# Near units' probabilities turned by VectorE and moved by DMA, with the order planned anew around the VectorE-GpSimd port

## The chip, the cores and the metric

One core of one Trainium2 chip. The metric is the device time of the program in microseconds. The kernel before took 573.14 us (median of three runs, 572.16 to 573.74).

## The reference

Block-sparse attention, then a channel mixer. q, k and v are (4, 8, 768, 64): 4 batches, 8 heads, 768 positions in 24 blocks of 32. A query block sees its own block and both neighbours, blocks 0 and 23, and three sampled blocks; query blocks 0 and 23 see everything.

```python
scores = np.where(mask, scale * q @ k.T, -1e9)
attn = np.exp(scores - scores.max(-1)); attn /= attn.sum(-1) + 1e-9
x = heads_side_by_side(attn @ v)                       # (4, 768, 512)
x_prev = shift_by_one_position(x)
xk = mu_k * x + (1 - mu_k) * x_prev;  xr = mu_r * x + (1 - mu_r) * x_prev
k = relu(xk @ w_k)                                     # (512, 1024)
out = sigmoid(xr @ w_r) * (k * k @ w_v)                # (1024, 512), (512, 512)
```

The three weights come as float64 and are made into float32 on the chip; q, k and v are float32.

## The kernel before

The work is cut into units and tiles. Units 0 to 3 (`wide_unit`) are query blocks 0 and 23 of one batch each, against all 768 keys. Units 4 to 25 (`near_unit`) are one query block each, n = 1 to 22, of all four batches, against eight key blocks per batch; a near unit is worked in two groups (`gi`) of four heads. The mixer has 12 tiles of two query blocks; tile t needs the near units of its two blocks.

A near group goes through these steps. TensorE makes the scores `s` (L559). VectorE takes the row maxima `nm` (L567, L569). ScalarE takes exp in four instructions into `p` (L539), with the columns of a 128 x 128 part so interleaved that part x holds the keys of all four batches. `turn` (L515) then transposes `p` in two halves: four TensorE transposes against the identity into PSUM tile `t` (L523), and one copy of 128 x 512 into `pt`, by ScalarE (L527) or VectorE (L529; one of four halves, from unit 6 on). TensorE multiplies `pt`, 32 x 32 at a time, by the values `VA` into `o` (L585). `finish` divides by the sums (L657 to L661), transposes (`tx`, L668) and copies into `xt` (L685, L688).

A mixer tile: `split_x` makes `xr` and `xk` (differences by GpSimd L740, VectorE L743, ScalarE L750, GpSimd L752) as high and low halves; `gate` (L776), `hidden` (L794) and `values` (L823) are TensorE products of three terms each; ScalarE and GpSimd square (L807 to L811), VectorE multiplies by the gate (L831), SyncE stores (L834). Products, `t` and `tx` share two PSUM banks, tag "m". `weight` makes each of 20 weight pieces float32 (L373 to L392) and splits it (L396, L400).

Nothing is in a fixed order: each piece is given to `Plan.add` with an engine, an estimated duration, a rank (a due time in us, such as `UNIT_AT`, `MIX_AT` plus an offset such as `O_PV`), what it reads and writes, and buffers. `Plan.order` simulates the engines: on each engine, of the pieces that could start within `NEAR` ns of the first, the one of lowest rank is taken. The pieces are then emitted in that order, and every engine, SyncE's DMA queue too, runs its own in order. All loads and stores are issued by SyncE.

```python
HOP = {"PE": 260, "ACT": 100, "DVE": 170, "POOL": 170, "SP": 60}
late, op, at = min((c for c in cand if c[0] <= first + NEAR),
             key=lambda c: (c[1].rank - STAY * (c[1].table is not None and c[1].table == now_on), c[1].seq))
```

Of the kernel before, what the change touches and what calls it, by code (L numbers as in the profile page):

```python
# [81 lines left out]
class Op:  # L82
    __slots__ = ("engine", "ns", "lag", "fn", "rank", "deps", "users", "bufs", "end", "start", "table", "seq", "waits", "release", "size", "code", "dmas")


class Plan:


    HOP = {"PE": 260, "ACT": 100, "DVE": 170, "POOL": 170, "SP": 60}
    SWITCH = {"ACT": 1300, "PE": 110}  # L90
    SAME = {"PE": 0}
    RING, RING_POOL, RATE, DONE, DONE_POOL = 650, 1000, 370, 670, 2600
# [7 lines left out]
    def add(self, engine, ns, rank, fn, reads=(), writes=(), lag=0, table=None, release=0.0, size=0, code=0, dmas=1):  # L100
# [36 lines left out]
    CHUNK, FIRST, FETCHED, FLIGHT = 258, 214, 5200, 8  # L137

    def feed(self, op, at, ns):

        end, left, since = at, op.code, self.crossed
        upto = self.upto
        while left >= upto:
            end += ns * upto / op.code
            end = since = max(end, since + self.FETCHED)
            left -= upto
            upto = self.CHUNK
        return end + ns * left / max(op.code, 1), since, upto - left

    WINDOW, LOW, HIGH = 3413.0, 0.45, 0.75  # L150
# [39 lines left out]
    def order(self):  # L190
        free, table, avail = {}, {}, {}
        self.crossed, self.upto = 0.0, self.FIRST
        self.now, self.busy, self.speed, self.window_end = 0.0, 0.0, 1.0, self.WINDOW
        queue_free, lands = 0.0, [0.0] * self.FLIGHT
        for op in self.ops:
            if not op.waits:
                avail.setdefault(op.engine, []).append(op)
# [3 lines left out]
        while len(placed) < len(self.ops):  # L201
            best = None
            for engine, ops in avail.items():
                now = free.get(engine, 0.0)
                cand = []
                for op in ops:
                    at = max(now, op.release)
                    if op.size and engine != "POOL":
                        at = max(at, lands[-self.FLIGHT])
                    for d in op.deps:  # L210
                        at = max(at, d.end + (self.HOP[d.engine] if d.engine != engine else self.SAME.get(engine, 60)) + d.lag)
# [7 lines left out]
                    if at is not None:  # L219
                        cand.append((at + (self.feed(op, at, op.ns)[0] - at - op.ns if op.code else 0.0), op, at))  # L220
                if cand:
                    first = min(c[0] for c in cand)
                    now_on = table.get(engine)
                    late, op, at = min((c for c in cand if c[0] <= first + NEAR),
                                 key=lambda c: (c[1].rank - STAY * (c[1].table is not None and c[1].table == now_on), c[1].seq))
# [20 lines left out]
            for buf in op.bufs:  # L246
# [7 lines left out]
                if not buf.left:  # L254
                    self.queues[buf.tag][1].append((op.end + op.lag + self.HOP[op.engine], buf.slot))
            for u in op.users:
                u.waits -= 1
                if not u.waits:
                    avail.setdefault(u.engine, []).append(u)
            placed.append(op)  # L260
        return sorted(placed, key=lambda o: o.start)

# [9 lines left out]
def block_sparse_attention_channel_mix(  # L272
# [18 lines left out]
    plan.add(POOL, 400, -9, lambda: make_identity(nc, ident.ap), writes=[(ident,)])  # L291
# [10 lines left out]
    def mask_setup():  # L302
# [35 lines left out]
        plan.add(DVE, 4000, PICK + 3, pack, reads=[(number,), (con,)], writes=[(r,), (e,), (packed,)])  # L338
# [19 lines left out]
    def weight(i, owner, key, dst, src, rank):  # L358
        f = buf([P, 512], F32, "zr", 3, f"wf{i}")
        if wide:  # L360
# [7 lines left out]
            if i in MAG_POOL:  # L368
                plan.add(POOL, 1950, rank, lambda: nc.gpsimd.tensor_scalar(
                    out=mag.ap, in0=raw.ap[:, :, 1].bitcast(F32), scalar1=2.0**-111, scalar2=None, op0=ALU.mult),  # L370
                    reads=[(raw,)], writes=[(mag,)])
            else:
                plan.add(ACT, 690, rank, lambda: nc.scalar.activation(  # L373
# [16 lines left out]
            plan.add(DVE, 500, rank, shift, reads=[(mag,)], writes=[(mag,)])  # L390
            plan.add(DVE, 800, rank, sign, reads=[(mag,), (raw,)], writes=[(mag,)])
            plan.add(DVE, 800, rank, tail, reads=[(mag,), (raw,)], writes=[(f,)])  # L392
        else:
            plan.add(SP, ISSUE, rank, lambda: nc.sync.dma_start(f.ap, src), writes=[(f,)], size=262144)
        if i in HI_POOL:
            plan.add(POOL, 700, rank, lambda: nc.gpsimd.tensor_copy(dst()[:, 0, :], f.ap), reads=[(f,)], writes=[(owner, (0, key))])  # L396
        else:
            plan.add(ACT, 520, rank, lambda: nc.scalar.copy(dst()[:, 0, :], f.ap), reads=[(f,)], writes=[(owner, (0, key))])
        plan.add(POOL, 1300, rank,
                 lambda: nc.gpsimd.tensor_tensor(out=dst()[:, 1, :], in0=f.ap, in1=dst()[:, 0, :], op=ALU.subtract),  # L400
                 reads=[(f,), (owner, (0, key))], writes=[(owner, (1, key))])
# [113 lines left out]
    def turn(parts, name, rank, engine=ACT):  # L515

        tp = buf([P, 4, P], F32, "m", M_BUFS, f"t{name}", ps)
        pt = buf([P, 4, P], F32, "pt", PT_BUFS, f"pt{name}")
        many = len(parts)

# [4 lines left out]
        plan.add(PE, 98 * many, rank, tr, reads=[(ident,), *[(p, x // P // 3 if wide_p(p) else x // 256) for p, x in parts]], writes=[(tp,)], code=2 * many)  # L525
        if engine == ACT:
            plan.add(ACT, 200 + 0.75 * P * many, rank + 0.1, lambda: nc.scalar.copy(pt.ap[:, 0:many], tp.ap[:, 0:many]), reads=[(tp,)], writes=[(pt,)])  # L527
        else:
            plan.add(DVE, 150 + 1.05 * P * many, rank + 0.1, lambda: nc.vector.tensor_copy(out=pt.ap[:, 0:many], in_=tp.ap[:, 0:many]), reads=[(tp,)], writes=[(pt,)])  # L529
        return pt  # L530
# [6 lines left out]
    def direct_exp(p, out, s, view, nm, rank, key, turned=lambda x: x):  # L537
        width = out.stop - out.start
        plan.add(ACT, 262 + 0.83 * width, rank, lambda: nc.scalar.activation(  # L539
            turned(p.ap[:, out]), view(), AF.Exp, bias=nm(), scale=SCALE), reads=[(s,), key[0]], writes=[(p, key[1])], table="exp")  # L540

    def near_unit(at, q, first, o, t0, kind):

        c0 = first // QB
        for gi in range(2):
# [4 lines left out]
            p = buf([P, 4 * 256], F32, "p", P_BUFS, f"p{name}")  # L550
# [20 lines left out]
            plan.add(DVE, N_TOP, t1 + O_MAX[kind], top, reads=[(s,)], writes=[(nm,)])  # L571
            for i in range(4):
# [3 lines left out]
                           lambda one: one.rearrange("p (c x j) -> p c j x", c=2, j=QB))  # L576
            pts = [turn([(p, x * P) for x in range(4 * k, 4 * k + 4)], f"{name}_{k}", t1 + O_TR[kind], DVE if at >= TURN_FROM and (gi, k) in TURN_DVE else ACT) for k in range(2)]

            def pv(pts=pts, gi=gi):
                for row in range(2):  # L580
                    for a in range(2):
                        i, h = 2 * a + row, 4 * gi + 2 * a + row
                        for g in range(2):
                            for j in range(QB):
                                nc.tensor.matmul(  # L585
                                    o[gi].ap[ROWS[j], i * DV : (i + 1) * DV], pts[row].ap[:, 2 * a + g, ROWS[j]],
                                    VA.ap[:, c0 + g, j, h * DV : (h + 1) * DV], start=(g == 0), stop=(g == 1), skip_group_check=True)

            plan.add(PE, N_PV, t1 + O_PV[kind], pv, reads=[(x,) for x in pts] + [(VA, *PLACE(c0, *range(QB)), *PLACE(c0 + 1, *range(QB)))],
                     writes=[(o[gi], 0)], table="values", code=128)  # L590

    def wide_unit(b, q, o, t0, kind):

        W = S // 2
        for i in range(2):
# [4 lines left out]
            for k in range(2):  # L600
# [11 lines left out]
                plan.add(PE, N_WIDE_S, t1, mm, reads=[(q,), (KA, *wide_key_parts(b, i), *wide_key_parts(b, i + 2))], writes=[(s,)], table="wide", code=16)  # L612
                plan.add(DVE, 930, t1 + O_MAX[kind], lambda s=s, k=k, nm=nm: nc.vector.tensor_reduce(
# [6 lines left out]
            plan.add(DVE, 220, t1 + O_MAX[kind], top, reads=[(nm, 0, 1)], writes=[(nm, 2)])  # L620
            pp = [buf([P, 4 * 256], F32, "p", P_BUFS, f"p{name}_{row}") for row in range(2)]
            wide_ps.update(pp)
            for k in range(2):
                for row in range(2):
                    direct_exp(pp[row], slice(k * W, (k + 1) * W), ss[k], lambda s=ss[k], row=row: s.ap[:, row, 0:W],
                               lambda nm=nm, row=row: nm.ap[:, 2, row : row + 1], t1 + O_EXP[kind], ((nm, 2), k))
            parts = [(p, n * P) for p in pp for n in range(6)]
            pts = [turn(parts[4 * k : 4 * k + 4], f"{name}_{k}", t1 + O_TR[kind] + 0.05 * k) for k in range(3)]
            for row in range(2):

                def pv(row=row, i=i, pts=pts):
                    c = 2 * i + row
                    for n in range(6):
                        x = 6 * row + n
                        c1, part = wide_place(b, n)
                        for a in range(2):
                            h = 4 * a + c
                            for e in range(2):
                                nc.tensor.matmul(
                                    o.ap[ROWS[2 * a + e], c * DV : (c + 1) * DV], pts[x // 4].ap[:, x % 4, ROWS[2 * a + e]],  # L640
# [3 lines left out]
                plan.add(PE, N_WIDE_PV, t1 + O_PV[kind], pv, reads=[(pts[k],) for k in (row, row + 1)]  # L644
# [3 lines left out]
    def finish(at, members, o, parts, rank):  # L648
# [3 lines left out]
        for i in range(len(o)):  # L652
# [7 lines left out]
            plan.add(DVE, 366, rank, recip, reads=[(o[i], *parts)], writes=[(R, i)])  # L660
            plan.add(DVE, 420, rank, lambda i=i, each=each: nc.vector.tensor_tensor(  # L661
# [8 lines left out]
        plan.add(PE, 200 * len(o), rank, tr, reads=[(x, *range(len(o))), (ident,)], writes=[(tp,)], code=4 * len(o))  # L670
        n = members[0][1]
        if not n:
# [9 lines left out]
            plan.add(ACT, 1100, rank, put, reads=[(tp,)], writes=[(xt[0], ("w", b)), (xt[NTILE - 1], ("w", b))])  # L682
            return
        to = tile_of(n // 2)
        plan.add(ACT, 600, rank, lambda: nc.scalar.copy(  # L685
            to.ap[:, :, n % 2, :, 1:], tp.ap.rearrange("p c (b x) -> p c b x", b=B)), reads=[(tp,)], writes=[(to, n)])
        then = tile_of((n + 1) // 2)
        plan.add(ACT, 240, rank + 0.1, lambda: nc.scalar.copy(  # L688
# [9 lines left out]
    def attention():  # L698
        for t in (0, NTILE - 1):
            tile_of(t)  # L700
        plan.add(POOL, 50, -5, lambda: nc.gpsimd.memset(xt[0].ap[:, :, 0, :, 0:1], 0.0), writes=[(xt[0], ("z", 0))])
# [261 lines left out]
```

## Time and profile before

| what | value |
|---|---|
| median of three runs | 573.14 us (572.16 to 573.74) |
| span of the profiled execution, first to last instruction | 570.2 us |
| mean granted TensorE clock | 0.987 of 2.4 GHz |
| read and written in HBM | 78.60 MB, 6.29 MB |

The profiled execution has no own time beside its span; the median of the runs is 2.9 us above the span. In the views, PE is TensorE's matmuls, PEld its weight loads, DVE VectorE, ACT ScalarE, POOL GpSimd, SPq SyncE's queue. The chain follows the work that ended last back from the end, at each step to what released it. Matmuls overlap one another, so that a piece of the chain tells better than a mean duration what an instruction costs TensorE.

### The profile page before, as it was taken

The page shows a single profiled execution, that of the slowest core. Times are in us where ns is not written, and L with a number is a line of the kernel's source. Part 1 is how long each engine was busy: PE and PEld are TensorE (multiplying, and loading weights), DVE is VectorE, ACT ScalarE, POOL GpSimd, SP SyncE. Part 2 cuts the span into 40 slices and gives each one's busy share as a digit, 9 for nine tenths or more (in the row PEclk, how much of TensorE's full clock was granted, in tenths as well). Part 3 has the DMA queues.
Part 4 walks back from the last instruction along what each step waited for, and adds up shares of the span by engine and source line. Part 5 has one row for each costly group of instructions (what it writes and reads, how often), then busy time and mean ns, then how long its engine had stood idle before and what let it go on. Part 6 is the DMA issues. An engine that isn't in the chain of part 4 may idle for free.

```text
span 570.2 us, 18311 instructions
## 1 busy us (share of the span) xinstructions
PE 537.7 (94%) x7724; PEld 438.5 (77%) x7724; DVE 269.6 (47%) x533; ACT 325.2 (57%) x612; POOL 291.0 (51%) x359
## 2 busy tenths in 40 slices
PE   6788778979999999999999999999999999999997
PEld 2454556856887798897798798887877989889886
DVE  0877998887445353434424524433452242142411
ACT  0676687768478468467464756546564356424330
POOL 0430456887266066346066285373383663448752
PEclk9799899999999999999999999999999999999999
DMA  8999899773653553362651804135510302110001
GB/s 314 395 398 342 295 343 352 260 228 94 192 182 95 172 164 116 112 189 76 189 167 29 278 24 157 36 100 166 169 39 20 95 19 84 32 39 1 20 20 38
DMA packets 34183, 86.09 MB, mean 151 GB/s; under 512 B 5010, under 2 KB 5780, under 8 KB 31124
## 3 DMA queue, kind: packets, MB, share of 16 engines
q1 hardware_dynamic: 34100, 84.92, 44.5%
q8 instruction: 61, 1.00, 0.7%
q14 instruction: 22, 0.18, 0.1%
HBM read 78.60 MB, written 6.29 MB: 149 GB/s over the span
## 4 chain that ended last, share of the span: by engine, by line
PE 80%; DVE 9%; DMA 4%; ACT 2%; POOL 2%; issue 2%; SPq 0%; DVEq 0%; ACTq 0%
PE v L823 23%; PE o L585 6%; PE s L559 6%; PE t L523 6%; PE r_0p L776 5%; PE h_1p L794 5%; PE h_3p L794 5%; PE h_0p L794 5%; PE h_2p L794 5%; PE r_1p L776 4%; PE tw L523 2%; PE sw L608 2%; DVE nm L567 2%; PE tx L668 2%; DMA raw<-w_v 1%
## 5 line engine op out<-in xcount | busy, mean ns | idle before, releaser
L823 PE MATMUL v<-wv,k 128*128 128x512 f32 (+1 forms) x600 | 145.0, 391 | 0.0
L823 PEld LDWEIGHTS v<-wv,k 128*128 128x128 f32 x600 | 106.8, 188 | 22.8 <-DVE x L661 0.8
L539 ACT ACTIVATE p<-s,nm 128x256 f32<-128x256 f32 x176 | 104.1, 728 | 18.1 <-DVE nm L569 13.8
L567 DVE TENSOR_REDUCE nm<-s 128x4 f32<-128x1024 f32 x44 | 53.6, 1219 | 16.1 <-PE s L559 16.1
L523 PE MATMUL t<-ident,p 128*128 128x128 f32 x352 | 54.6, 278 | 4.7 <-ACT z L783 2.4
L585 PE MATMUL o<-VA,pt 128*32 128x65 f32 x2816 | 49.9, 222 | 6.7 <-ACT pt L527 4.0
L585 PEld LDWEIGHTS o<-VA,pt 128*32 128x32 f32 x2816 | 42.3, 109 | 16.9 <-issue 9.7
L752 POOL TENSOR_TENSOR xr<-xr_1f,xr 128x256 fp32r<-128x256 f32 x24 | 17.7, 737 | 70.8 <-ACT xr L750 70.8
L523 PEld LDWEIGHTS t<-ident,p 128*128 128x128 f32 x352 | 40.2, 140 | 16.1 <-ACT z L783 2.9
L527 ACT COPY pt<-t 128x512 f32<-128x512 f32 x68 | 40.7, 604 | 18.7 <-PE t L523 15.7
L559 PE MATMUL s<-KA,q 64*32 64x256 f32 x1408 | 46.5, 387 | 1.6 <-DVE wf L386 1.2
L743 DVE SCALAR_TENSOR_TENSOR xr_1f<-xr_1d,mk,xt 128x128 f32<-128x128 f32 x48 | 17.9, 372 | 55.9 <-POOL xr L752 46.3
L831 DVE SCALAR_TENSOR_TENSOR z<-v,z 128x512 f32<-128x512 f32 (+1 forms) x25 | 16.8, 670 | 50.1 <-PE v L823 50.0
L685 ACT COPY xt<-tx 128x512 f32<-128x512 f32 x22 | 13.0, 591 | 42.1 <-PE tx L668 42.0
L794 PE MATMUL h_0p<-xk,wk 128*128 128x256 f32 x288 | 37.0, 282 | 0.0
L776 PE MATMUL r_1p<-wr,xr 128*128 128x512 f32 x144 | 36.4, 400 | 0.6 <-ACT h_3k L807 0.6
L794 PE MATMUL h_3p<-xk,wk 128*128 128x256 f32 x288 | 36.4, 281 | 0.0
L743 DVE SCALAR_TENSOR_TENSOR xr_0f<-xr_0d,mk,xt 128x128 f32<-128x128 f32 x48 | 20.3, 424 | 34.0 <-POOL xk L752 13.9
L776 PE MATMUL r_0p<-wr,xr 128*128 128x512 f32 x144 | 36.4, 400 | 0.0
L794 PE MATMUL h_1p<-xk,wk 128*128 128x256 f32 x288 | 36.3, 281 | 0.0
L794 PE MATMUL h_2p<-xk,wk 128*128 128x256 f32 x288 | 36.3, 280 | 0.0
L794 PEld LDWEIGHTS h_0p<-xk,wk 128*128 128x128 f32 x288 | 35.1, 188 | 0.7
(139 smaller groups left out, 940.1 us busy)
## 6 DMA issues: line engine op xcount, KB each, us to landing
VA<-vt SPq DMA_DIRECT2D x93, 260.0 KB, 3.8
KA<-kt SPq DMA_DIRECT2D x90, 256.0 KB, 3.7
VA<-vw SPq DMA_DIRECT2D x24, 260.0 KB, 6.1
KA<-kq SPq DMA_DIRECT2D x16, 384.0 KB, 6.7
out<-z SPq DMA_DIRECT2D x23, 256.0 KB, 2.2
q<-qt SPq DMA_DIRECT2D x22, 256.0 KB, 4.3
early_w<-w_k SPq DMA_DIRECT2D x8, 512.0 KB, 6.4
raw<-w_v SPq DMA_DIRECT2D x8, 512.0 KB, 5.0
```

What stands on the lines that cost most here:

```text
L523: nc.tensor.transpose(tp.ap[:, i, :], p.ap[:, x : x + P], ident.ap)
L527: plan.add(ACT, 200 + 0.75 * P * many, rank + 0.1, lambda: nc.scalar.copy(pt.ap[:, 0:many], tp.ap[:, 0:many]), reads=[(tp,)], writes=[(pt,)])
L539: plan.add(ACT, 262 + 0.83 * width, rank, lambda: nc.scalar.activation(turned(p.ap[:, out]), view(), AF.Exp, bias=nm(), scale=SCALE), read ...
L559: nc.tensor.matmul(s.ap[ROWS[j], row, a * 256 : (a + 1) * 256].rearrange("p (n x) -> p n x", x=BLK), q.ap[half, (hp * QB + j) * BLK : (hp ...
L567: nc.vector.tensor_reduce(out=nm.ap.rearrange("p (r a) -> p r a", r=2), in_=s.ap.rearrange("p r (a x) -> p r a x", a=2), axis=AX.X, op=ALU ...
L585: nc.tensor.matmul(o[gi].ap[ROWS[j], i * DV : (i + 1) * DV], pts[row].ap[:, 2 * a + g, ROWS[j]], VA.ap[:, c0 + g, j, h * DV : (h + 1) * DV ...
L743: nc.vector.scalar_tensor_tensor(out=parts(f.ap[:, i, :]), in0=parts(d.ap), scalar=mk.ap[:, which, c : c + 1], in1=cols(c, 1), op0=ALU.mul ...
L752: plan.add(POOL, 80 + 2.4 * MIX * tw, rank + O_MIX, lambda f=f, cs=cs: nc.gpsimd.tensor_tensor(out=dst.ap[:, 1, cs], in0=f.ap, in1=dst.ap[ ...
L776: nc.tensor.matmul(pr.ap[:, 0:512], xr.ap[:, a, c, :], wr.ap[:, w, c, :], start=(c == 0 and m == 0), stop=(c == CC - 1 and m == 2))
L794: nc.tensor.matmul(ph.ap[:, ff * TT : (ff + 1) * TT], wk.ap[:, w, c, f * P : (f + 1) * P], xk.ap[:, a, c, :], start=(c == 0 and m == 0), s ...
L823: nc.tensor.matmul(pv.ap[:, 0:width], k2.ap[:, a, f, i * P : (i + 1) * P], wv.ap[:, w, f, cs], start=(f == 0 and m == 0), stop=(f == FC - ...
L831: plan.add(DVE, 150 + 1.05 * width, done, lambda pv=pv, cs=cs: nc.vector.scalar_tensor_tensor(out=z.ap[:, cs], in0=pv.ap[:, 0:width], scal ...
```

## The change

In near units 8 to 25 `near_move` replaces both calls of `turn`: the exps write `p` in another column order, one VectorE instruction transposes every 32 x 32 square of the 128 x 1024 tile into `r`, and four DMAs on SyncE's queue, one per batch, spread the 32 partitions of a batch over all 128 partitions of `pt`. The products `o` then read `pt` as before, in the same number. `p` and `r` share the tag "p" (four buffers); `pt` has two buffers of 128 x 1024 where it had three of 128 x 512.

Units 0 to 7 keep `turn`; which halves VectorE copies is now a list of names (`TURN_DVE`, 13 of 40). Of the 20 weight pieces GpSimd casts 10 and ScalarE the other 10 (GpSimd cast all 20), and VectorE does 8 of the 20 subtractions (GpSimd did all). In tiles 2, 3, 4, 8, 9, 10 and 11 VectorE does the differences of L740.

The planner has one delay per pair of engines, costs by pair of TensorE modes, new DMA figures, a `port` that GpSimd instructions and some of VectorE's hold one at a time, and a `STAY` that now favours the mode in which TensorE is. All durations, ranks and lead times are new.

```diff
-    HOP = {"PE": 260, "ACT": 100, "DVE": 170, "POOL": 170, "SP": 60}
-    SWITCH = {"ACT": 1300, "PE": 110}
-    RING, RING_POOL, RATE, DONE, DONE_POOL = 650, 1000, 370, 670, 2600
+    HOP = {
+        "PE": {"PE": 0, "ACT": 200, "DVE": 215, "POOL": 240, "SP": 240},
+        "ACT": {"PE": 265, "ACT": 146, "DVE": 147, "POOL": 192, "SP": 180},
+        "DVE": {"PE": 231, "ACT": 119, "DVE": 119, "POOL": 151, "SP": 115},
+        "POOL": {"PE": 200, "ACT": 120, "DVE": 79, "POOL": 124, "SP": 120},
+        "SP": {"PE": 100, "ACT": 60, "DVE": 60, "POOL": 60, "SP": 60},
+    }
+    MODES = {"turn": 0, "whole": 1, "scores": 2, "values": 3}
+    CHANGE = ((0, -81, 93, 93), (0, 0, 92, 92), (137, 137, 0, 137), (115, 115, 113, 0))
+    RING, RING_POOL, RATE, DONE, DONE_POOL = 1200, 1500, 395, 700, 2600
...
+        op.port, op.ready = max((ns if engine == "POOL" else port) - self.BUBBLE, 0), 0.0
...
+            elif op.port:
+                op.end = port = max(at + ns - op.port, port) + op.port
...
+            if at >= MOVE_FROM:
+                near_move(at, gi, s, nm, c0, o, t1, kind)
+                continue
...
+    def near_move(at, gi, s, nm, c0, o, t1, kind):
+        name = f"{at}_{gi}"
+        p = buf([P, QB, 2, 4, BLK], F32, "p", P_BUFS, f"p{name}")
+        for i in range(4):
+            row, a = divmod(i, 2)
+            plan.add(ACT, 365, t1 + O_EXP[kind], lambda row=row, a=a, i=i: nc.scalar.activation(
+                p.ap[:, :, :, i, :].rearrange("p j c x -> p c j x"),
+                s.ap[:, row, a * 256 : (a + 1) * 256].rearrange("p (c j x) -> p c j x", c=2, j=QB),
+                AF.Exp, bias=nm.ap[:, i : i + 1], scale=SCALE), reads=[(s,), (nm,)], writes=[(p, i)], table="exp")
+        r = buf([P, QB, 2, 4, BLK], F32, "p", P_BUFS, f"r{name}")
+        plan.add(DVE, N_TURN, t1 + O_TURN, lambda: nc.vector.transpose(
+            out=r.ap.rearrange("p j c i x -> p (j c i x)"), in_=p.ap.rearrange("p j c i x -> p (j c i x)")),
+            reads=[(p, *range(4))], writes=[(r,)], port=N_TURN)
+        pt = buf([P, B, 2, 4, BLK], F32, "pt", PT_BUFS, f"pt{name}")
+        def move():
+            for b in range(B):
+                nc.sync.dma_start(pt.ap[:, b].rearrange("p c i x -> p (c i x)"),
+                                  r.ap[ROWS[b]].rearrange("p j c i x -> p j (c i x)"))
+        plan.add(SP, B * ISSUE, t1 + O_MOVE, move, reads=[(r,)], writes=[(pt,)], size=MOVE_SIZE, dmas=B)
...
+                                o[gi].ap[ROWS[j], i * DV : (i + 1) * DV], pt.ap[:, j, g, 2 * row + a, :],
...
-ISSUE, FETCH, FIND, GATHER = 470, 735, 640, 1000
-XT_BUFS, P_BUFS, PT_BUFS, M_BUFS = 3, 4, 3, 2
-HI_POOL = frozenset(range(20))
-DIF_DVE = frozenset()
-NEAR, STAY, STORE = 34.076, -1.502, 639.005
+ISSUE, FETCH, FIND = 420, 735, 640
+XT_BUFS, P_BUFS, PT_BUFS, M_BUFS = 3, 4, 2, 2
+MOVE_FROM, MOVE_SIZE, N_TURN = 8, 560000, 1135
+NEAR = 62.891
+STAY = 12.056
+HI_POOL = frozenset([0, 1, 5, 12, 13, 14, 16, 17, 18, 19])
+LO_DVE = frozenset([0, 3, 6, 9, 12, 14, 18, 19])
+DIF_DVE = frozenset([2, 3, 4, 8, 9, 10, 11])
```

## Rows read from the trace of the kernel before

**Rows 1.** The page: the span, and busy time, share and instructions of each engine.

```profile
span 570.2 us, 18311 instructions
...
PE 537.7 (94%) x7724; PEld 438.5 (77%) x7724; DVE 269.6 (47%) x533; ACT 325.2 (57%) x612; POOL 291.0 (51%) x359
```

**Rows 2.** The page's 40 slices: granted TensorE clock in tenths.

```profile
PEclk9799899999999999999999999999999999999999
```

**Rows 3.** By stretch, us: length; PE, PEld, DVE, ACT, POOL busy; clock, DMA, GB/s.

```profile
0.00:25.00 25.00, 17.76 (x168) 7.70 (x168) 10.19 (x16) 8.19 (x15) 4.70 (x11) 0.80 0.94 349
25.00:50.00 25.00, 21.10 (x427) 12.85 (x420) 18.28 (x35) 17.23 (x38) 8.25 (x8) 1.00 1.03 383
50.00:75.00 25.00, 20.05 (x565) 13.31 (x571) 24.24 (x53) 18.04 (x37) 9.24 (x9) 0.93 0.92 312
75.00:100.00 25.00, 20.03 (x527) 14.57 (x515) 21.57 (x44) 18.84 (x40) 15.03 (x21) 1.00 0.96 349
100.00:125.00 25.00, 21.23 (x429) 18.11 (x418) 20.64 (x35) 16.80 (x33) 22.23 (x23) 1.00 0.77 252
...
150.00:200.00 50.00, 49.27 (x742) 40.50 (x732) 22.89 (x48) 32.46 (x62) 21.45 (x28) 1.00 0.51 159
```

**Rows 4.** The chain from 150 us to the end: shares by engine and line.

```profile
by line: PE v L823 29.4%; PE o L585 7.8%; PE r_0p L776 7.4%; PE h_1p L794 7.4%; PE h_3p L794 7.3%; PE h_0p L794 7.3%; PE h_2p L794 7.3%; PE t L523 6.9%; PE s L559 6.7%; PE r_1p L776 6.0%; PE tx L668 2.3%; DVE nm L567 0.8%; DVE nm L569 0.5%;
```

**Rows 5.** Pieces of the chain, 470 to 495 us: start us, length us, what.

```profile
478.29 1.05 PE o L585 x64
479.34 3.03 PE h_1p L794 x24
482.37 0.44 PE t L523 x4
...
483.88 0.59 PE t L523 x4
484.47 2.75 PE h_2p L794 x24
```

**Rows 6.** Groups of lines from 150 us on: busy us, mean ns | idle before, releaser.

```profile
L523 PE MATMUL t<-ident,p 128*128 128x128 f32 x256 | 39.3, 276 | 2.4 <-ACT z L783 2.4
```

**Rows 7.** The same view of the whole span.

```profile
L567 DVE TENSOR_REDUCE nm<-s 128x4 f32<-128x1024 f32 x44 | 53.6, 1219 | 16.1 <-PE s L559 16.1
...
L527 ACT COPY pt<-t 128x512 f32<-128x512 f32 x68 | 40.7, 604 | 18.7 <-PE t L523 15.7 <-PE o L585 3.0
...
L529 DVE COPY pt<-t 128x512 f32<-128x512 f32 x20 | 13.8, 689 | 6.9 <-PE o L585 5.7 <-PE t L523 0.9
```

**Rows 8.** Waits of TensorE from 150 us on: total us, times, longest.

```profile
PE t L523 <- ACT z L783: 2.4, 3, 1.1
```

**Rows 9.** Waits of TensorE before 150 us.

```profile
PE o L585 <- ACT pt L527: 4.0, 2, 3.4
```

**Rows 10.** Pieces of the chain, 100 to 150 us.

```profile
115.60 1.70 POOL wv L400
...
119.26 1.11 DVE wmag L378
```

**Rows 11.** Line 378: durations in ns, min/median/max.

```profile
L378 DVE TENSOR_SCALAR wmag<-wmag x20: 404/428/1503, 16.0 to 128.7; 128x512 int32<-128x512 int32 x20
```

**Rows 12.** Waits of SyncE's queue: total us, times, longest.

```profile
SPq L452 <- PE o L585: 135.9, 19, 14.3
SPq L834 <- DVE z L831: 121.7, 14, 27.2
```

**Rows 13.** DMA issues of the page: count, KB each, median us to landing.

```profile
KA<-kt SPq DMA_DIRECT2D x90, 256.0 KB, 3.7
```

**Rows 14.** Line 834: issue durations in ns, min/median/max, and us to landing.

```profile
L834 SPq DMA_DIRECT2D out<-z x25: 332/344/1388, 144.6 to 567.4; - x25
...
DMA to landing us min/median/max: 1.7/2.1/4.7
```

More of the change, by code (lines that the diff above doesn't have):

```diff
@@ L98, in __init__, with add @@
         self.queues = {}
-    def add(self, engine, ns, rank, fn, reads=(), writes=(), lag=0, table=None, release=0.0, size=0, code=0, dmas=1):
+    def add(self, engine, ns, rank, fn, reads=(), writes=(), lag=0, table=None, release=0.0, size=0, code=0, dmas=1, port=0):
         op = Op()
@@ L147, in feed @@
             upto = self.CHUNK
-        return end + ns * left / max(op.code, 1), since, upto - left
-    WINDOW, LOW, HIGH = 3413.0, 0.45, 0.75
+        return end + op.ns * left / op.code - at - op.ns
     def turn_window(self):
@@ L202, in order @@
             best = None
[L203 to L207, printed above, removed]
+            for engine in engines:
+                now, now_on = free[engine], table.get(engine)
+                cand, first = [], None
+                for op in avail[engine]:
+                    at = max(now, op.ready)
                     if op.size and engine != "POOL":
                         at = max(at, lands[-self.FLIGHT])
-                    for d in op.deps:
-                        at = max(at, d.end + (self.HOP[d.engine] if d.engine != engine else self.SAME.get(engine, 60)) + d.lag)
                     for buf in op.bufs:
@@ L569, in top @@
                 nc.vector.tensor_scalar(out=nm.ap, in0=nm.ap, scalar1=-SCALE, scalar2=None, op0=ALU.mult)
-            plan.add(DVE, N_TOP, t1 + O_MAX[kind], top, reads=[(s,)], writes=[(nm,)])
+            plan.add(DVE, N_TOP, t1 + O_MAX[kind], top, reads=[(s,)], writes=[(nm,)], port=70)
+            if at >= MOVE_FROM:
+                near_move(at, gi, s, nm, c0, o, t1, kind)
+                continue
+            p = buf([P, 4 * 256], F32, "p", P_BUFS, f"p{name}")
             for i in range(4):
@@ L590, in near_unit, with pv @@
                      writes=[(o[gi], 0)], table="values", code=128)
+    def near_move(at, gi, s, nm, c0, o, t1, kind):
[17 more added lines that the diff above has]
+        plan.add(SP, B * ISSUE, t1 + O_MOVE, move, reads=[(r,)], writes=[(pt,)], size=MOVE_SIZE, dmas=B)
+        def pv():
+            for row in range(2):
+                for a in range(2):
+                    i, h = 2 * a + row, 4 * gi + 2 * a + row
+                    for g in range(2):
+                        for j in range(QB):
+                            nc.tensor.matmul(
+                                o[gi].ap[ROWS[j], i * DV : (i + 1) * DV], pt.ap[:, j, g, 2 * row + a, :],
+                                VA.ap[:, c0 + g, j, h * DV : (h + 1) * DV], start=(g == 0), stop=(g == 1), skip_group_check=True)
+        plan.add(PE, N_PV, t1 + O_PV[kind], pv, reads=[(pt,), (VA, *PLACE(c0, *range(QB)), *PLACE(c0 + 1, *range(QB)))],
+                 writes=[(o[gi], 0)], table="values", code=128)
@@ L618, in top @@
                 nc.vector.tensor_scalar(out=nm.ap[:, 2, :], in0=nm.ap[:, 2, :], scalar1=-SCALE, scalar2=None, op0=ALU.mult)
-            plan.add(DVE, 220, t1 + O_MAX[kind], top, reads=[(nm, 0, 1)], writes=[(nm, 2)])
+            plan.add(DVE, 262, t1 + O_MAX[kind], top, reads=[(nm, 0, 1)], writes=[(nm, 2)], port=150)
             pp = [buf([P, 4 * 256], F32, "p", P_BUFS, f"p{name}_{row}") for row in range(2)]
@@ L668, in tr @@
                 nc.tensor.transpose(tp.ap[:, c], x.ap[:, c * P : (c + 1) * P], ident.ap)
-        plan.add(PE, 200 * len(o), rank, tr, reads=[(x, *range(len(o))), (ident,)], writes=[(tp,)], code=4 * len(o))
+        plan.add(PE, 218 * len(o), rank, tr, reads=[(x, *range(len(o))), (ident,)], writes=[(tp,)], table="turn", code=4 * len(o))
         n = members[0][1]
@@ L780, in gate @@
             cs = (2 * half, 2 * half + 1)
[L781 removed]
+            plan.add(PE, 1400, rank + half * 1.3, lambda cs=cs: mm(cs),
                      reads=[(xr, *SPLIT), (wr, *[(a, c) for a in range(2) for c in cs])], writes=[(pr,)], code=12)
[L783 removed]
+        plan.add(ACT, 475, rank, lambda: nc.scalar.copy(z.ap, pr.ap[:, 0:512]), reads=[(pr,)], writes=[(z,)])
     def hidden(name, xk, k2, f2, last, rank):
```

200 lines of the change are left out of this document (113 added, 87 removed).

## The prediction

> **What bounds the kernel now.** I read the page first, then the stretches, then the chain of the later part, then the waits. TensorE is busy 94% of the span, the next engine 57% [rows 1]; since matmuls overlap, that alone proves little. The stretches split the run in two [rows 3]. Up to 125 us TensorE lacks 7.24, 3.90, 4.95, 4.97 and 3.77 us, together 24.8 us, while the DMA engines are over 90% busy for 100 us and VectorE works 84.7 of the 100 us from 25 to 125. From 150 us on TensorE is without gaps (49.27 of 50.00), at the full granted clock [rows 2, 3], and the chain there is nearly all TensorE [rows 4]: over 420 us the only wait of its matmuls is 2.4 us [rows 8]. In that part an instruction taken from TensorE is time taken from the span, as long as what remains arrives in time. In the first part it is not: there the chain runs through VectorE and GpSimd in turns, and one instruction of 0.43 us (median) takes 1.11 us behind a GpSimd instruction of 1.70 us [rows 10, 11].
>
> **Turns removed after 150 us.** Units 8 to 25 are 18 units of 2 groups of 2 turns: 72 of 88. From 150 us on the trace has 256 transposes [rows 6], so 64 turns, and they hold 6.9% of 420.2 us of chain [rows 4], 29.0 us or 0.45 us each. Not all of it is won. A turn costs 0.44 us in front of a product, and 0.59 us behind one; but a mixer piece straight behind a product takes 3.03 us, where behind a turn it takes 2.75 us [rows 5]. So a turn behind a product saves 0.59 + 2.75 - 3.03 = 0.31 us. I take 0.40 us, nearer to the more frequent kind: 64 x 0.40 = 25.6 us, bounds 64 x 0.31 = 19.8 and 29.0.
>
> **Turns removed before 150 us.** The other 8 lie where TensorE has gaps, two of them, 4.0 us together, in front of products that waited for a turn's copy [rows 9]: between nothing and 8 x 0.45 = 3.6 us; I take 1.8.
>
> **The way of a moved group.** Before, two turns of 0.45 us and two copies of 0.60 us [rows 7] led from the exps to the products. Now come a VectorE transpose of 128 x 1024, four issues and four landings. The trace has no such transpose: the nearest row of that size is the reduction, 1.22 us; at the rate of two columns it would be about the 0.69 us of the 128 x 512 copy, at half rate 2.44 us [rows 7]. I take 1.22. An issue of SyncE without a computed address takes 0.34 us, so four take 1.4 us, and a store of 256 KB lands 1.7 to 4.7 us later, median 2.1 [rows 14]; the loads' 3.8 us is within that [rows 13]. Together 1.2 + 1.4 + 2.1 = 4.7 us, at worst 7.3. The plan itself allows 1.135 + 0.115 + 4 x 0.42 + 1.2 + 560/395 + 0.7 + 0.1 = 6.35 us from the transpose's start to the products. The median fits with 1.6 us to spare, the slowest landing is 1.0 us late. TensorE takes its instructions in order, so a late transfer stops it and everything queued behind: gates, hidden, values, the next scores. I charge 0.1 us a group, 36 x 0.1 = 3.6 us; the bounds are nothing and 36 x 1.0 = 36 us.
>
> **SyncE's queue.** Each group puts four issues and a wait for VectorE in front of loads, and stands behind waits itself: SyncE waits 135.9 us in total for products before value loads and 121.7 us for stores [rows 12]. Loads behind a move had 2 to 14 us of such waits already and TensorE did not stop for them after 150 us, so I charge nothing beyond the 0.1 us. The 36 moves carry 36 x 0.524 = 18.9 MB; at the 349 to 383 GB/s of the full stretches that is 49 to 54 us of DMA time, where the share is 0.51 [rows 3].
>
> **Other engines.** VectorE gains 36 x 1.22 = 44 us, some 24 us of differences (7 tiles of 8 small ones and 4 large) and some 13 us of weights and copies, and loses the 18 copies of 0.69 us that it made in these units. From 270 us it comes to about 340 of 541, 63%; after 150 us it was at 22.9 of 50. ScalarE loses 54 copies (32 us), GpSimd the differences and half its weight work. All three stay below TensorE; the cover is that surplus of mixer work, and if it goes the cost is rival C.
>
> **The first part and the plan.** New work for VectorE there: 11 copies more (7.6 us) and 8 subtractions (about 5.5 us). If VectorE sets the end of this part, all 13.1 us are lost. Against this GpSimd loses 10 casts and 8 subtractions, and the plan now keeps the two engines off each other's port; if that halves TensorE's 24.8 us, 12.4 us are won. The 7.24 us of the start belong to loads, so I take 3 us won. The new STAY keeps TensorE in one mode: each return saved is worth 3.03 - 2.75 = 0.28 us; if half of the 72 score and value pieces lose theirs, 10 us, and at least nothing. I take 2.
>
> **Sum.** 570.2 - 25.6 - 1.8 - 3 - 2 + 3.6 = 541.4 us of span. The median of the runs is 2.9 us above the span, so 544 us.
>
> **Rivals.**
> A, the forecast, 544 us (534 to 554).
> B, the port was the real brake of the first part: 12.4 us instead of 3, and 10 for the modes instead of 2: 527 us. For it: the alternation in [rows 10]. Against: the DMA engines are full in the same 100 us.
> C, VectorE in order: a transpose of 1.22 us stands ahead of a reduction, a division or the z of a tile whose bank TensorE needs. If each costs TensorE one removed turn, 36 x 0.45 = 16 us come back: 560 us. Against: VectorE has half its time free.
> D, the other side: the moves land late. Each transfer reads 32 neighbouring partitions and writes 128, and no transfer of the trace reads so. If such a transfer runs at half the rate of the full stretch, 0.524 MB takes 2.74 us instead of 1.37 us at 383 GB/s [rows 3]; the plan allows 1.42. Then every product waits 1.37 us: 36 x 1.37 = 49 us in place of the 3.6, 590 us. It decides from (28.8 + 3.6) / 36 = 0.90 us a group. Against: the spare 1.6 us above covers it at the median landing; for it: that spare is only the plan's, and SyncE's waits come on top. The Trainium skill, "SBUF — State Buffer", section "Door 1: The DMA port swizzle", states the rule that makes this likely: 32 partitions reach 8 of the 16 ports, and at 1 MiB it gives 189 GB/s against 328 for all 128; by its rate the 0.524 MB would take an estimated 2.8 us. No row here shows it.
> E, it does not do what it says: stalls of 0.8 us a group eat the turns: 573 us.
>
> **Chances.** A 0.60, B 0.16, C 0.11, D 0.10, E 0.03. A measurement of this kernel can tell 0.3% (1.7 us) from no change. Faster is A, B and C: 0.87; the same E: 0.03; slower D: 0.10. The range reaches below to B and above past C, 526 to 563, and leaves out D, E and the ends.
>
> **What would show it.** Right: line 523 keeps 16 turns of units 4 to 7 (64 transposes) and those of the wide units; TensorE has no wait from 150 us on above a few us; VectorE's transpose takes 1.1 to 1.3 us; the last of four landings comes within 2 to 3 us. C would show as TensorE waiting for VectorE or for z; D as TensorE's products, L585 of before, waiting for a DMA into pt some 36 times, with landings above 4 us. B would show as TensorE busy over 22.5 of 25 us in each stretch from 25 to 125 us. The forecast is wrong if TensorE's busy time falls by 25 us or more but the span does not.

## The result and the profile after

The changed kernel takes 542.01 us (median of 4 runs, 539.1 to 544.91) against 572.77 us: ratio 0.947, 95% interval 0.943 to 0.951. The prediction was 544 us (534 to 554 for its rival A, 526 to 563 in all).

The page of the changed kernel, which answers to [rows 1]:

```profile
span 539.6 us, 17943 instructions
...
PE 504.0 (93%) x7436; PEld 413.9 (77%) x7436; DVE 331.4 (61%) x654; ACT 273.3 (51%) x555; POOL 236.6 (44%) x257
```

TensorE has 33.7 us less work and is still at 93%; its idle time went from 570.2 - 537.7 = 32.5 to 35.6 us. The span fell by 33.7 - 3.1 = 30.6 us. VectorE went from 47 to 61%, ScalarE from 57 to 51%, GpSimd from 51 to 44%. By stretch, columns as in [rows 3]:

```profile
0.00:25.00 25.00, 15.43 (x161) 7.34 (x161) 11.84 (x20) 6.62 (x11) 4.63 (x11) 0.90 0.94 353
25.00:50.00 25.00, 18.47 (x346) 10.87 (x342) 23.19 (x54) 13.63 (x28) 4.95 (x5) 0.83 0.98 353
50.00:75.00 25.00, 19.47 (x551) 13.13 (x543) 21.50 (x45) 19.97 (x39) 5.05 (x5) 1.00 0.99 350
75.00:100.00 25.00, 20.43 (x546) 14.27 (x550) 17.85 (x41) 20.75 (x49) 11.98 (x17) 1.00 0.91 301
100.00:125.00 25.00, 21.78 (x397) 19.43 (x376) 19.76 (x35) 14.19 (x27) 16.60 (x18) 0.93 0.75 266
125.00:150.00 25.00, 25.00 (x383) 19.23 (x390) 19.97 (x33) 14.93 (x29) 12.52 (x16) 1.00 0.60 168
150.00:200.00 50.00, 48.19 (x804) 41.09 (x796) 29.70 (x66) 25.34 (x55) 19.73 (x22) 1.00 0.79 241
```

After 125 us TensorE is full again. Before 125 us it lacks 9.57, 6.53, 5.53, 4.57 and 3.22 us, 29.4 us where it was 24.8. The loss lies in the first 50 us. VectorE's busy time in 25 to 50 us rose from 18.28 to 23.19 us. TensorE waits for the wide units' exps and copies; over the first 150 us (total us, times, longest):

```profile
PE sw L674 <- ACT pw L564: 9.6, 5, 4.1
PE o L707 <- DVE ptw L555: 5.8, 2, 4.7
```

Of the 9.6 us, 4.1 fall before 25 us and 5.2 between 25 and 50; of the 5.8 us, 4.7 and 1.1. The exps in turn wait for VectorE, in 25 to 50 us:

```profile
ACT pw L564 <- DVE nmw L684: 5.8, 3, 4.3
```

The lines that the change is about, from the groups of lines (busy, mean ns, count), as [rows 6, 7]:

```profile
L633 DVE STREAM_TRANSPOSE r<-p 128x1024 f32<-128x1024 f32 x36 | 44.6, 1240 | 4.9 <-ACT p L628 4.0 <-PE t L549 0.2
...
L549 PE MATMUL t<-ident,p 128*128 128x128 f32 x64 | 9.9, 282 | 2.0 <-ACT pt L553 1.5 <-DVE pt L555 0.5
```

The 36 transposes take 1.24 us each; 64 of the near units' 352 TensorE transposes are left. The move's issues and landings, as [rows 14], and TensorE's waits from 150 us on, as [rows 8]:

```profile
L640 SPq DMA_DIRECT2D pt<-r x144: 543/602/2127, 128.8 to 463.3; - x144
...
DMA to landing us min/median/max: 2.5/3.1/5.0
```

```profile
PE o L651 <- issue: 1.2, 2, 0.7
PE o L651 <- DMA pt<-r: 0.6, 2, 0.5
```

An issue takes 0.60 us and a landing 3.1 us, both more than I took; TensorE's products still wait only 0.6 us for `pt`.

### The profile page after: what moved, and what is told of

Same layout as the page of the kernel before. It is cut to its first block, busy times and chain, and to the rows that moved or that the text cites. A ratio compares the mean times of both kernels' runs of the same rounds, so it can differ in the third digit from the quotient of the medians.

```text
span 539.6 us, 17943 instructions
## 1 busy us (share of the span) xinstructions
PE 504.0 (93%) x7436; PEld 413.9 (77%) x7436; DVE 331.4 (61%) x654; ACT 273.3 (51%) x555; POOL 236.6 (44%) x257
## 4 chain that ended last, share of the span: by engine, by line
PE 82%; DVE 7%; DMA 3%; ACT 3%; issue 2%; POOL 1%; SPq 1%; ACTq 0%; POOLq 0%; DVEq 0%
PE v L891 23%; PE s L583 7%; PE h_1p L862 6%; PE h_3p L862 6%; PE h_2p L862 6%; PE r_1p L844 6%; PE o L651 6%; PE r_0p L844 6%; PE h_0p L862 6%; PE tx L736 2%; DMA KA<-kt 2%; PE sw L674 2%; DVE nmw L679 1%; DMA pt<-r 1%; PE warm L370 1%
## 5 line engine op out<-in xcount | busy, mean ns | idle before, releaser
L891 PE MATMUL v<-wv,k 128*128 128x512 f32 (+1 forms) x600 | 137.8, 387 | 0.0
L891 PEld LDWEIGHTS v<-wv,k 128*128 128x128 f32 x600 | 108.9, 188 | 25.0 <-issue 0.4
L628 ACT ACTIVATE p<-s,nm 128x256 f32<-128x256 f32 x144 | 58.1, 487 | 18.9 <-DVE nm L593 17.3
L633 DVE STREAM_TRANSPOSE r<-p 128x1024 f32<-128x1024 f32 x36 | 44.6, 1240 | 4.9 <-ACT p L628 4.0
L651 PEld LDWEIGHTS o<-VA,pt 128*32 128x32 f32 x2304 | 34.5, 109 | 9.3 <-issue 6.0
L651 PE MATMUL o<-VA,pt 128*32 128x65 f32 x2304 | 38.7, 221 | 2.1 <-issue 1.2
L862 PEld LDWEIGHTS h_0p<-xk,wk 128*128 128x128 f32 x288 | 36.8, 194 | 3.9 <-issue 3.0
L583 PEld LDWEIGHTS s<-KA,q 64*32 64x32 f32 x1408 | 25.0, 106 | 18.5 <-issue 6.1
L811 DVE SCALAR_TENSOR_TENSOR xr_1f<-xr_1d,mk,xt 128x128 f32<-128x128 f32 x48 | 17.7, 369 | 31.1 <-POOL xr L820 28.7
L820 POOL TENSOR_TENSOR xr<-xr_0f,xr 128x256 fp32r<-128x256 f32 x24 | 18.0, 748 | 40.3 <-ACT xr L818 40.0
L862 PEld LDWEIGHTS h_1p<-xk,wk 128*128 128x128 f32 x288 | 34.8, 188 | 0.7 <-issue 0.5
L862 PEld LDWEIGHTS h_3p<-xk,wk 128*128 128x128 f32 x288 | 34.7, 188 | 0.1
```

The source lines that it names most:

```text
L583: nc.tensor.matmul(s.ap[ROWS[j], row, a * 256 : (a + 1) * 256].rearrange("p (n x) -> p n x", x=BLK), q.ap[half, (hp * QB + j) * BLK : (hp ...
L628: plan.add(ACT, 365, t1 + O_EXP[kind], lambda row=row, a=a, i=i: nc.scalar.activation(p.ap[:, :, :, i, :].rearrange("p j c x -> p c j x"), ...
L633: plan.add(DVE, N_TURN, t1 + O_TURN, lambda: nc.vector.transpose(out=r.ap.rearrange("p j c i x -> p (j c i x)"), in_=p.ap.rearrange("p j c ...
L651: nc.tensor.matmul(o[gi].ap[ROWS[j], i * DV : (i + 1) * DV], pt.ap[:, j, g, 2 * row + a, :], VA.ap[:, c0 + g, j, h * DV : (h + 1) * DV], s ...
L811: nc.vector.scalar_tensor_tensor(out=parts(f.ap[:, i, :]), in0=parts(d.ap), scalar=mk.ap[:, which, c : c + 1], in1=cols(c, 1), op0=ALU.mul ...
L820: plan.add(POOL, 137 + 2.12 * MIX * tw, rank + O_MIX, lambda f=f, cs=cs: nc.gpsimd.tensor_tensor(out=dst.ap[:, 1, cs], in0=f.ap, in1=dst.a ...
```

## The experiments

Each is measured beside the kernel before, whose median is 572 to 573 us in each set.

| run | what differs | us | ratio to before (95%) |
|---|---|---|---|
| turns back | changed kernel, 8 transposes per moved group whose result nothing reads | 572.34 | 0.997 (0.994 to 1.001) |
| old plan, moves | before, with moves only | 585.96 | 1.022 (1.016 to 1.028) |
| old plan, longer move planned | the same, move told longer | 584.43 | 1.024 (1.016 to 1.031) |
| old plan, moves, ranks searched | the same, new ranks | 564.93 | 0.989 (0.981 to 0.996) |
| new plan, no moves | changed kernel, TensorE turns | 589.04 | 1.028 (1.025 to 1.032) |
| new plan, no moves, ranks searched | the same, new ranks and split | 578.06 | 1.010 (1.007 to 1.014) |
| planner's rate 393 | a new order, nothing else | 549.87 | 0.961 (0.957 to 0.965) |
| port off | planner without the port | 559.73 | 0.976 (0.973 to 0.979) |
| port off, ranks searched | the same, new ranks | 553.05 | 0.967 (0.962 to 0.972) |
| port on, ranks searched | its control | 544.05 | 0.950 (0.948 to 0.953) |
| transpose without port | planner only | 543.87 | 0.948 (0.943 to 0.953) |
| wide source | transfers read 128 partitions | 539.89 | 0.943 (0.939 to 0.946) |

**Is it TensorE's time?** The turns are put back where TensorE's order, and everybody else's, stays the same.

```diff
         def pv():
+            for _ in range(8):
+                nc.tensor.transpose(o[gi].ap[:, 384:512], ident.ap, ident.ap)
...
-            o = [buf([P, 4 * DV], F32, "o", 2, f"o{i}_{k}", ps) for k in range(1 if wide_one else 2)]
+            o = [buf([P, 512], F32, "o", 2, f"o{i}_{k}", ps) for k in range(1 if wide_one else 2)]
```

> The changed kernel in its own order, with eight TensorE transposes of the identity, into columns of the o bank that nothing reads, put back in front of the products of every moved group; copies, moves and all other engines stay as they are. Theory T (the gain is TensorE time taken from an engine that is full): four transposes cost 0.44 us in the chain of before, so 36 x 0.88 = 31.7 us come back, 570 to 575 us. Theory P (the gain comes from the new plan and the new split of the other engines, TensorE has slack): at most 553 us.

The gain is gone: 572.34 us, beside 573.06 us for the kernel before in the same set. The span, and the pieces of the chain (start, length, what) around one unit's two groups:

```profile
span 570.7 us, 18503 instructions
```

```profile
250.78 0.87 PE o L647 x8
251.66 1.05 PE o L653 x64
252.71 1.02 PE o L647 x8
```

Eight transposes cost 0.87 us behind a mixer piece and 1.02 us behind a product. The span grew by 570.7 - 539.6 = 31.1 us, 0.43 us per turn (the medians by 30.3 us). TensorE was full, and its time is the price; the edit touches no copy and no move, and widens the PSUM buffers of `o` only to make room for the idle results.

**Do the moves pay without the new plan?**

> The kernel before with nothing but the moves: old planner, old ranks, old split of VectorE, ScalarE and GpSimd; the transpose is ranked just behind the exps, the move where the turn was, pt in two buffers of 128 x 1024. Theory T: most of the gain is there without the new plan, 543 to 555 us. Theory P: at least 565 us. Theory L (moves need a plan that knows their time, or they land late): above 556 us with TensorE waiting for pt.

They do not: 585.96 us, slower than before. T falls; the bounds of P and L hold, but none of the three had foreseen a loss, and L's sign, TensorE waiting for `pt`, is nearly absent. TensorE's waits from 150 us on:

```profile
PE tx L712 <- DVE x L705: 18.5, 13, 5.5
PE s L559 <- DMA KA<-kt: 5.8, 2, 4.0
PE o L627 <- DMA pt<-r: 2.3, 2, 1.3
PE s L559 <- DMA q<-qt: 2.1, 1, 2.1
```

The landings are not the trouble, 2.3 us. TensorE waits above all for `x`, the division. It also waits 7.9 us for loads of keys and queries, which share SyncE's queue with the moves; the kernel before had no such wait there [rows 8]. VectorE's and then TensorE's instructions in order of time (start, length, line, tiles, count, idle before) show one such place:

```profile
211.56 0.18 DVE L702 RECIPROCAL R<-R 128x4 f32<-128x4 f32 x1
211.77 1.25 DVE L609 STREAM_TRANSPOSE r<-p 128x1024 f32<-128x1024 f32 x1
212.94 0.39 DVE L705 TENSOR_TENSOR x<-o,R 128x256 f32<-128x256 f32 x1
```

```profile
209.44 1.10 PE L627 MATMUL o<-VA,pt 128*32 128x65 f32 x58 [0.96 <-DMA pt<-r]
...
213.38 0.69 PE L712 MATMUL tx<-ident,x 128*128 128x128 f32 x2 [2.47 <-DVE x L705]
213.72 5.34 PE L838 MATMUL h_2p<-xk,wk 128*128 128x256 f32 x24
218.89 2.89 PE L838 MATMUL h_3p<-xk,wk 128*128 128x256 f32 x24
```

A transpose of 1.25 us stands between the reciprocal and the division; TensorE's `tx` waits 2.47 us, and all the mixer's work queues behind it. That is rival C's mechanism. More time is lost behind the wait: `h_2p` takes 5.34 us where the next 24 take 2.89. The granted clock is the third number from the end in these stretches:

```profile
200.00:213.00 13.00, 9.95 (x240) 8.16 (x238) 8.92 (x16) 5.53 (x13) 8.29 (x10) 0.96 0.80 229
213.00:219.00 6.00, 5.62 (x27) 5.63 (x28) 1.57 (x3) 2.13 (x6) 0.00 (x0) 0.52 0.92 298
```

TensorE had stood still twice just before, for 0.96 and 2.47 us; then, from 213 to 219 us, the granted clock is 0.52, about the level of 1.2 GHz instead of 2.4. That the waits brought the clock down is read from this order in time; no run tests it by itself.

Telling the old planner of a longer move does not mend it:

```diff
-MOVE_FROM, MOVE_SIZE, N_TURN = 8, 560000, 1135
+MOVE_FROM, MOVE_SIZE, N_TURN = 8, 1100000, 1240
```

> The kernel before with the moves, as in the run at 586 us, but with the old planner told a longer move (size 1,100,000 instead of 560,000, 1.46 us more) and a transpose of 1.24 us. Theory late (the old plan lets VectorE stand before a tile whose move has not landed, and the division and TensorE's tx queue behind): the waits of VectorE for pt landings fall from 26 us to below 10 and the time to 555 to 570 us. Rival (the old plan is wrong elsewhere, in its delays and durations): above 578 us.

584.43 us: the theory "late" falls, and so does its sign. VectorE still waits 17.6 us for landings in front of a transpose (its buffer is one that an earlier move is reading), where the theory asked for less than 10, and TensorE's wait for the division stays:

```profile
DVE r L609 <- DMA pt<-r: 17.6, 8, 6.8
PE tx L712 <- DVE x L705: 17.8, 16, 2.9
```

With ranks searched anew (some 13,000 random steps of `UNIT_AT`, `MIX_AT`, the offsets and so on, kept when the planner's own order ended no later), the old planner comes to 564.93 us:

> The kernel before with the moves under the old planner and the old split, as in the run at 586 us, with ranks searched anew for the moves. If the moves only needed ranks made for them: 543 to 556 us. If the old planner's delays and durations are too wrong for them: 560 to 580 us, with TensorE waiting for VectorE's divisions (tx) or for pt.

```profile
PE 521.3 (92%) x7436; PEld 415.2 (74%) x7436; DVE 304.1 (54%) x551; ACT 279.7 (50%) x560; POOL 290.2 (51%) x359
```

So 21 of the 44 us between 586 and 542 were ranks made without moves (TensorE's waits for the division are gone from 150 us on), and 23 us remain with the old planner and the old split. Of the 24.0 us between the two spans, 563.6 and 539.6 us, TensorE's busy time makes up 17.3, 521.3 against 504.0 us for the same 7436 matmuls. A part of that shows in the timelines from 150 us on: this run goes straight from a product or a score to a mixer piece 37 times, the changed kernel 7 times. At the 0.28 us per return of the prediction, the 30 more are an estimated 8 us. The rest stays open.

**Does the new plan pay without the moves?**

```diff
-MOVE_FROM, MOVE_SIZE, N_TURN = 8, 560000, 1135
+MOVE_FROM, MOVE_SIZE, N_TURN = 26, 560000, 1135
-O_TR = [15.566, -690.855, -120.328, -8.083]
+O_TR = [15.566, 15.566, -120.328, -8.083]
```

The second pair of lines gives the later units the turn offset of the early ones; with the first pair alone the planner finds no order at all, so that there is no kernel to time.

> The changed kernel with all near units turned by TensorE as before and no moves, under the new planner, ranks and split; the turn's offset of the later units is set to 15.566, that of the early ones. If the new plan were worth something by itself beside the moves: at most 553 us. If the gain needs the turns off TensorE: 565 to 580 us, since putting the 288 transposes back into the same order has cost 30 us and here the copies come back too.

> All near units turned by TensorE, no moves, under the new planner, as in the run at 589 us, but with ranks and split of work searched anew for this mix by some 20,000 random steps on the planner's own order. Theory T (the moves' worth is TensorE's turns): even with a fitted order 567 to 580 us, no faster than before by more than 1%. Theory P (the new planner is worth something by itself once its ranks fit): at most 556 us.

589.04 us, above both ranges named for it, and 578.06 us with ranks and split searched anew, as its theory T had it. TensorE's busy time is back, here in the second run:

```profile
PE 543.9 (94%) x7724; PEld 443.8 (77%) x7724; DVE 307.8 (53%) x656; ACT 316.9 (55%) x596; POOL 229.9 (40%) x252
```

The plan alone shows no gain; my search may have left a few us. Between the fitted runs the moves are worth 578 - 542 = 36 us under the new planner and 573 - 565 = 8 us under the old. Each of these orders comes from one search, so the two figures hold to a few us at best.

**What is the port worth in the plan?** First the port was taken out of the planner, then the price of any new order was measured.

```diff
-        op.port, op.ready = max((ns if engine == "POOL" else port) - self.BUBBLE, 0), 0.0
+        op.port, op.ready = 0, 0.0
```

> The changed kernel with the port taken out of the planner: the order is planned as if GpSimd and VectorE never held each other up. Theory T with my small term for the first part: 541 to 547 us. The rival that the port order is what pays: at least 549 us, with VectorE instructions of the weights waiting behind GpSimd again and TensorE idle more than 35 us in the first 150.

> The changed kernel with the planner's DMA rate at 393 instead of 395 bytes per ns, and nothing else: a new order from the same ranks, as a measure of what any new order costs. Theory port (the 17.7 us of the run without the port are the port's): 540 to 546 us here. Theory order (the ranks fit one order, and any other costs about as much): 553 to 562 us.

559.73 us without the port; but a rate of 393 instead of 395, which says nothing new, gives 549.87 us. Both theories named there are too simple: a new order from old ranks can by itself cost 7.9 of the 17.7 us. It need not: the run that lets the transpose hold no port, below, is another new order from the same ranks and costs 1.9 us. Without the port TensorE's idle time grows most in the first part, 150 - 113.2 = 36.8 us there against 150 - 120.6 = 29.4 us, as the rival had said:

```profile
0.00:150.00 150.00, 113.21 (x2092) 75.99 (x2093) 104.95 (x207) 82.56 (x164) 46.62 (x58) 0.87 0.79 273
```

So ranks were searched for the planner without the port, and, as a control, for one with it:

> The changed kernel planned without the port, as in the run at 560 us, with the same split of work but ranks searched anew for that planner. Theory order (the 17.7 us were the price of ranks that fit another order, as 7.8 us were in the run with a hardly changed rate): 540 to 548 us. Theory port (a plan that does not know of the port loses to VectorE and GpSimd holding each other up): 551 to 560 us, with VectorE's instructions of the weights at over 1 us again.

> The control to the run planned without the port (553 us): the same split, the planner with its port (VectorE's transpose alone holds none, as in the run at 544 us), and ranks searched anew in the same way and for as long. Theory port (a plan that knows the port is better by some 10 us): 538 to 546 us. Theory order (any order whose ranks were searched in this way comes out near 553, and the changed kernel's was a lucky one): 549 to 556 us. It is also the version that may beat the changed kernel, by 2 us at most.

553.05 us (550.95 to 556.0) and 544.05 us (542.67 to 544.74): 9.0 us apart, each where theory port had put it. It is one search on either side; how far two searches for the same planner differ was not measured without the port, and with it the two orders on record, 542 and 544 us, lie 2 us apart. Page, and stretches of 150 us, of the run without the port:

```profile
PE 511.1 (93%) x7436; PEld 415.2 (75%) x7436; DVE 342.0 (62%) x654; ACT 272.1 (49%) x555; POOL 235.4 (43%) x257
```

```profile
0.00:150.00 150.00, 121.88 (x2231) 82.29 (x2232) 116.86 (x222) 89.10 (x180) 57.17 (x70) 0.93 0.83 290
150.00:300.00 150.00, 143.02 (x2340) 119.91 (x2342) 93.44 (x187) 74.06 (x159) 59.60 (x58) 1.00 0.75 218
```

and of the control:

```profile
PE 506.0 (93%) x7436; PEld 414.7 (77%) x7436; DVE 325.3 (60%) x654; ACT 273.9 (51%) x555; POOL 236.7 (44%) x257
```

```profile
0.00:150.00 150.00, 122.13 (x2364) 84.67 (x2364) 115.11 (x226) 90.34 (x182) 58.35 (x71) 0.93 0.88 304
150.00:300.00 150.00, 146.86 (x2356) 124.59 (x2346) 93.53 (x198) 81.05 (x169) 63.18 (x64) 1.00 0.74 221
```

The same 654 VectorE instructions take 342.0 us without and 325.3 us with the port in the plan: 16.7 us more for the same work. But VectorE's time is not the price by itself, for the changed kernel, with 331.4 us, is no slower than the control. Of the 9.0 us between the spans (550.9 and 541.9), 3.8 are idle time of TensorE between 150 and 300 us, 143.02 against 146.86. Another 5.1 are a longer busy time of TensorE for the same 7436 matmuls, 511.1 against 506.0, and how these hang on the port stays open. TensorE is busy as long in the first part (121.88 and 122.13 us), but gets through 2231 matmuls there against 2364. The sign that theory port named shows weakly: of the 20 instructions of L399, the weights' first step on VectorE, the longest takes 1.08 us without and 0.62 us with the port, and the median 0.42 us in both. The control does not beat the changed kernel.

**Does the transpose need the port?**

```diff
-            reads=[(p, *range(4))], writes=[(r,)], port=N_TURN)
+            reads=[(p, *range(4))], writes=[(r,)])
```

> The changed kernel, but the planner lets VectorE's transpose hold no port, since it took 1.21 to 1.25 us in all 36 places, beside GpSimd work or not. If the transpose and GpSimd don't hold each other up: the transpose still at 1.21 to 1.25 us, GpSimd's durations unchanged, 538 to 546 us for a good order, up to 555 if a new order by itself costs. If they do: transposes or GpSimd instructions of over 2 us beside one another, and above 546 us.

543.87 us, and the transposes' durations (min/median/max ns) do not move:

```profile
L633 DVE STREAM_TRANSPOSE r<-p x36: 1224/1245/1247, 129.8 to 459.3; 128x1024 f32<-128x1024 f32 x36
```

It neither waits for GpSimd nor holds it up: in the timeline 22 of the 36 run beside a GpSimd instruction, and GpSimd's instructions beside them are no longer than the others (the 5 of L879 1.30 us on average, the other 43 1.33 us). The Trainium skill, "SBUF — State Buffer", section "Who interferes with whom", says so of VectorE instructions with one SBUF input outside the two-port modes; the run agrees (1.22 to 1.25 us in all 36 places). Line 378, one input too but of a form that the same section of the Trainium skill counts among those that can take both ports, went from 0.40 to 1.50 us [rows 11].

**Do 32 source partitions halve the rate?**

```diff
-                                  r.ap[ROWS[b]].rearrange("p j c i x -> p j (c i x)"))
+                                  r.ap[:, b].rearrange("p c i x -> p (c i x)"))
```

> The changed kernel in its own order, but each of the four transfers of a move takes its 128 pieces of 1 KB from 128 partitions instead of four from each of 32; what lands in pt is therefore another part of the probabilities. Rival D's rule (32 neighbouring partitions give half the rate): the landing falls from 3.1 us by 0.3 us or more, and the DMA share from 150 to 300 us falls. Otherwise the landing stays at 2.9 to 3.3 us. The time stays at 540 to 546 us either way, since TensorE waits for pt some 2 us in all.

539.89 us. Landings, and 150 to 300 us, in this run and then in the changed kernel:

```profile
DMA to landing us min/median/max: 2.0/2.9/5.6
```

```profile
150.00:300.00 150.00, 147.35 (x2359) 125.19 (x2352) 93.31 (x201) 80.08 (x170) 65.03 (x67) 1.00 0.71 225
```

```profile
150.00:300.00 150.00, 147.30 (x2384) 124.57 (x2369) 92.91 (x199) 79.74 (x169) 64.93 (x66) 1.00 0.77 225
```

The landing falls by 0.2 us, less than the 0.3 of rival D's rule, and the DMA share by 0.06. Some 75 transfers, 18.75 groups, lie in the stretch: 0.06 x 150 / 18.75 = 0.48 us of DMA time a group (the shares are rounded), against the 1.37 us of half a rate. A narrow source costs something, about a third of what the rule gives here, and TensorE does not see it (147.35 and 147.30 us busy).

## Why the prediction was right

**Turns.** Right, and under-sized: 25.6 + 1.8 = 27.4 us foretold, 31.1 us measured by putting them back. I had counted 8 turns into the part with gaps; in the new order the first move is issued at 128.8 us, so all 72 lie where TensorE is full. Per turn it is 0.43 us, not 0.40, a difference of little weight beside the 5.8 us over which the four runs of the changed kernel spread.

**The way of a move.** The sum was wrong, the conclusion right. Issues of 0.60 us, not 0.34, and a landing of 3.1 us, not 2.1, make 1.24 + 2.4 + 3.1 = 6.7 us instead of 4.7: no spare against the 6.35 us that I read from the planner's figures. A store into HBM was the wrong neighbour for this transfer. TensorE's idle time after 150 us nevertheless went only from 5.8 to 6.2 us, for which I had charged 3.6: products stand late enough in the order, and wait 0.6 us for `pt`. (The loads' landing that I gave as 3.8 us is 3.7 in [rows 13].)

**SyncE, VectorE.** As foretold: no wait of TensorE for a load after 150 us, VectorE at 331 of the "about 340" us. VectorE's total hit only because two misses cancel: the differences (L808) take 39.9 us where I had put 24, while instructions that both kernels run became shorter, those of L378, L382, L386 and L569 from 65.6 to 48.6 us (now L399, L403, L407 and L593, in the same numbers).

**The first part.** Wrong in sign: 3 us won foretold, 4.6 us lost up to 125 us, 1.9 us regained up to 150. Of the loss 2.3 us lie in the first 25 us, which I had put down to loads, and 2.6 in 25 to 50. That is less than the first of my two bounds, and its reason is another: of VectorE's work in 25 to 50 us only four copies (2.7 us) and one subtraction (0.7 us) are new there, while some 5 us are index arithmetic (L337 to L357) that the new order brings forward to 24 us, from 51 us before. My reading of [rows 10] was off as well: GpSimd's 1.70 us end at 117.30, and the VectorE instruction of 1.11 us starts at 119.26, beside another GpSimd instruction (L809, 1.06 us from 119.02).

**Modes.** The 2 us were not separated, and their premise was wrong. The kernel before goes straight from a product or a score to a mixer piece only 9 times from 150 us on, since a turn mostly stands between; the changed kernel does so 7 times. There was hardly a return to save. Returns can come when the turns go: the old planner's searched order with moves has 37 of them, its unsearched order only 3, but that one waits for the division instead.

**The sum.** With the turns back the span is 570.7 us against 570.2 us before, so everything but the turns comes to about nothing: 0.5 us lost by the spans, 0.7 us won by the medians, 572.34 against 573.06. My other terms promised 3 + 2 - 3.6 = 1.4 us. By the spans the turns came out 3.7 us better and the rest 1.9 us worse; that the span missed by only 541.4 - 539.6 = 1.8 us is luck in part. The 2.9 us that I added to the span were too many as well: the profiled execution took 541.39 us with a span of 539.6, and the other profiled executions show about the same 1.8 us.

**Rivals.** B did not come: TensorE is busy 15.4 to 21.8 us in each stretch up to 125 us, not 22.5. D's premise is a third of its size. C did not come in the changed kernel, but it is what happens to the moves under the old plan before its ranks are searched anew. E is out.

**What I missed** is what the plan is for. I gave it 5 us; alone it shows no gain, but under the old planner the moves bring some 8 us instead of some 36, and the one order searched without the port loses 9. My terms added up parts that hold only together. Which part of the planner does how much is not shown: the delays, the costs of changing modes and the new durations were never taken out one by one.

## What to carry to other kernels

On an engine that is full, count what leaves it by the pieces of the chain, and check by putting that work back without using its result: one run tells whether the time was its. A step moved to an in-order engine must be judged by what stands behind it there: VectorE had half its time free, and one transpose of 1.25 us in the wrong place still stopped TensorE for 2.47 us, and behind it the granted clock stood at half. Where an order is searched, measure a meaningless new order as well, better several, before a loss is put down to the edit: two further orders from the same ranks cost 1.9 and 7.9 us here.

## What the runs showed of the hardware

A 128 x 1024 float32 transpose by squares takes VectorE 1.21 to 1.25 us, much as a reduction of that size does (1.22 us), beside GpSimd work or not. A 128 KB transfer within SBUF, from 32 partitions to 128, took 0.60 us to issue and 3.1 us to land (medians); a store of 256 KB took 0.34 and 2.1 us. Why the issue takes longer is not shown. With all 128 partitions as its source such a transfer landed in 2.9 us.
